# Polynomial-sketch attention and a cosine router: 36 blocks of tokens in place of 41, last parts of experts in shared blocks, and another order of the early work

## The chip, the cores and the metric

The kernel runs on one core of a Trainium2 chip. The core has a matrix engine (TensorE, PE in the profile), a vector engine (VectorE, DVE), a scalar engine (ScalarE, ACT), a general engine (GpSimd, POOL) and a queue engine for transfers (SyncE, SP). Matmuls read the on-chip memory SBUF and write the accumulation memory PSUM, in banks of 512 fp32 numbers per partition; every tile has up to 128 partitions. Measured is the time of one execution on the device in microseconds, lower is better. All data are fp32 unless a line says bf16.

## The reference

Two stages. The first is linear attention with a product sketch; its result is handed, token by token, to a router that sends each token to one of 8 experts, each a two-layer network.

```python
batch, n_heads, seq, head_dim = (4, 4, 1088, 32);  r = 8
def phi(x):                                   # 64 features of a row of 32
    a = einsum('rd,bhsd->bhsr', S1, x)
    b = einsum('rd,bhsd->bhsr', S2, x)
    return einsum('bhsi,bhsj->bhsij', a, b).reshape(..., r * r)
q_p, k_p = phi(q), phi(k)
kv  = einsum('bhsf,bhsd->bhfd', k_p, v)       # sum over all keys
z   = sum(k_p, axis=2)
x   = einsum('bhsf,bhfd->bhsd', q_p, kv) / (einsum('bhsf,bhf->bhs', q_p, z)[..., None] + 1e-6)
x   = x.transpose(0, 2, 1, 3).reshape(4352, 128)          # tokens

logits = normalized(x) @ normalized(expert_emb).T / tau   # 8 experts
expert_idx = argmax(logits, axis=1)
gate = softmax(logits)[expert_idx]
for e in range(8):                            # w1: 8 x 128 x 1024, w2: 8 x 1024 x 128
    out[mask_e] = gate * (relu(x[mask_e] @ w1[e]) @ w2[e])
```

How many tokens an expert gets is known only when the router has run.

## The kernel before

The two halves of the batch are m = 0 and m = 1. A half is cut into 17 tiles of 128 rows, in groups of 4, 4, 4 and 4 + 1. Everything is written as steps with a tick and a rank; the ticks are emitted in order, so every engine has a fixed order of work. In ticks 0 to 3 keys and queries of the first half are prepared, in 4 to 7 its results are formed beside the keys of the second half, and so on.

Loads, in the order of the transfer queue (k, q and v have different layouts: q is cut with its own stride):

```python
    for m in range(NM):
        k_sb[m] = rows_p.tile([P, H, 2, NK, D], F32, tag="rows", name=f"k{m}")
        q_sb[m] = rows_p.tile([P, H, NC, D], F32, tag="rows", name=f"q{m}")
        load_k(m, 0)
        if m == 0:
            load_q(0, 0, 8)
        load_v(m, 0)
        load_k(m, 1)
        if m == 0:
            nc.sync.dma_start(emb_sb[:], emb)
            nc.sync.dma_start(tau_sb[:], bass.AP(tensor=tau.tensor, offset=tau.offset, ap=[[0, E], [1, 1]]))
            load_q(0, 8, NC)
        load_v(m, 1)
        load_rest(m)
        load_q_rest(m)
    load_q(1, 0, NC)
```

w2 of an expert comes in pieces of 512 B (128 numbers):

```python
    def load_w2(e):
        nc.sync.dma_start(w2_sb[:, e], w2[e].rearrange("(f p) d -> p f d", p=P))
```

The sketch of a tile (two linear maps of each row) and the products. `u` chooses the half of the output partitions. Keys and queries of a tick share one PSUM bank, of which there is one:

```python
    def sketch(ps, t, n):

        for u in range(2):
            r = slice(u * HALF, (u + 1) * HALF)
            if n == 1:
                nc.tensor.matmul(ps[r, :H * 2 * R], t[:, r], Sblk.rearrange("p g r -> p (g r)"), start=True, stop=True)
            else:
                for h in range(H):
                    nc.tensor.matmul(ps[r].rearrange("p (g h r) -> p g h r", h=H, r=2 * R)[:, :, h],
                                     t[:, h * P + u * HALF:h * P + (u + 1) * HALF], Sblk, start=True, stop=True)
        return ps[:, :n * H * 2 * R].rearrange("p (g t r) -> p g t r", t=2, r=R)

    def second(ab, n, tag):
        b = tile_of(n, [P, n * H, R], tag)
        nc.scalar.copy(b, ab[:, :, 1])
        return b

    def features(ab, b, n, tag):
        t = tile_of(n, [P, n, H, R * R], tag)
        nc.vector.tensor_mul(t.rearrange("p j h (i k) -> p (j h) i k", i=R),
                             ab[:, :, 0].unsqueeze(3).broadcast_to([P, n * H, R, R]),
                             b.unsqueeze(2).broadcast_to([P, n * H, R, R]))
        return t

    def ab_bank(tick, n):

        if (tick, n) not in ab_ps:
            ab_ps[tick, n] = ps_small()[:, :2 * P] if n == 1 else ps_one("ab")
        return ab_ps[tick, n]
```

The sum over keys, and the query side: the products `qp` are turned (`tr_qp`) and, for the first half, kept turned in the place that w2 of experts 4 to 7 gets later (`held`):

```python
                    for p in range(2):
                        for u in range(2):
                            h = 2 * p + u
                            vo = v_rest[m][i][:, h] if rest else v_sb[m][:, h, c]
                            to_ones = (H - h) * D if rest else ((H - h) * 2 * NK - c) * D
                            nc.tensor.matmul(
                                acc[m][u * HALF:(u + 1) * HALF, i, p], s["kp"][:, c - c0, h],
                                bass.AP(tensor=vo.tensor, offset=vo.offset,
                                        ap=[list(vo.ap[0]), [to_ones, 2], [1, D]]),
                                start=p == 0 and c == 0, stop=rest, skip_group_check=True)
...
        def tr_qp():
            ps = ps_big() if n > 1 else ps_small().rearrange("p (b n) -> p b n", b=2)
            for j in range(n):
                for p in range(2):
                    nc.tensor.transpose(ps[:, p, j * P:(j + 1) * P],
                                        s["qp"][:, j, 2 * p:2 * p + 2].rearrange("p h f -> p (h f)"), ident)
            s["qpT"] = held[:, c0 // 4] if m == 0 and n > 1 else tile_of(n, [P, 2, w], "qpT")
            nc.scalar.copy(s["qpT"], ps[:, :, :w])

        def nd():
            ps = ps_big().rearrange("p b (u n) -> p (b u) n", u=2) if n > 1 else ps_small().unsqueeze(1)
            W = 2 * COLS
            for j in range(n):
                for i in range(2):
                    for p in range(2):
                        nc.tensor.matmul(
                            ps[i * HALF:(i + 1) * HALF, j, p * W:(p + 1) * W],
                            s["qpT"][:, p, j * P + i * HALF:j * P + (i + 1) * HALF],
                            kz[m][:, i, p].rearrange("p h d -> p (h d)"), start=True, stop=True)
            s["hs"] = ps[:, :n, :2 * W].rearrange("p n (h d) -> p n h d", h=H)
```

The router finds each token's expert and place, `mark` and `table` build the lists of tokens by block, and `write` stores the rows of x in device memory, in one buffer for the first half and one for all. Blocks of 128 tokens belong to one expert each. Every expert can leave one block partly filled, so their number is

```python
NBLK = (N + E * (P - 1)) // P                              # (4352 + 8*127)//128 = 41
EARLY = (NM * NC * P // 2 - E * (P - 1) + P - 1) // P      # 10, known from the first half alone
LATE = NBLK - EARLY                                        # 31
```

A block fetches its rows by an indirect gather, turns them, copies the weights of its expert (chosen by a register) to a fixed place, and runs two layers:

```python
    def turn(i):
        ps = ps_small()
        nc.tensor.transpose(ps[:, :P], xs[i][:, :DM], ident)
        xT[i] = work.tile([P, P], F32, tag="xTb", name="xTb")
        nc.vector.tensor_copy(xT[i], ps[:, :P])

    def weights(i):
        t, j = of(i)

        both = (mybir.EngineType.DVE, mybir.EngineType.Activation)
        e = nc.values_load(exp_i[t][0:1, j:j + 1], engines=both[:2 - t], min_val=0, max_val=E - 1,
                           skip_runtime_bounds_check_because="a count of experts, clamped to the last one")
        wb[i] = rows_p.tile([P, 2, F], F32, tag="rows", name="wb")
        nc.vector.tensor_copy(wb[i][:, 0], w1_sb[:, bass.ds(e, 1)].rearrange("p o f -> p (o f)"))
        w2 = w2_sb[:, bass.ds(e, 1)].rearrange("p o f d -> p (o f d)")
        if t == 0:
            nc.scalar.copy(wb[i][:, 1], w2)
        else:
            nc.vector.tensor_copy(wb[i][:, 1], w2)
...
    def up(i):
        ps = ps_big()
        hT[i] = work.tile([P, 2, 512], F32, tag="kp", name="hT")
        x, w = xT.pop(i), wb[i][:, 0]
        for u in range(2):
            for j in range(4):
                f = 4 * u + j
                nc.tensor.matmul(ps[:, u, j * P:(j + 1) * P], w[:, f * P:(f + 1) * P], x, start=True, stop=True)
        nc.scalar.activation(hT[i], ps, ACT.Relu)
...
    def down(i):
        ps = ps_one(("acc", "ab")[i % 2])[:, :DM]
        h, w = hT.pop(i).rearrange("p u n -> p (u n)"), wb.pop(i)[:, 1].rearrange("p (f d) -> p f d", d=DM)
        for f in range(NF):
            nc.tensor.matmul(ps, h[:, f * P:(f + 1) * P], w[:, f], start=f == 0, stop=f == NF - 1)
        y = work.tile([P, DM], F32, tag="y", bufs=3, name="y")
        nc.scalar.activation(y, ps, ACT.Copy, scale=gate.pop(i)[:, 0:1])
        xs.pop(i)
        t, j = of(i)
        nc.gpsimd.indirect_dma_start(
            out=out[:, :], out_offset=bass.IndirectOffsetOnAxis(ap=dst_i[t][:, j:j + 1], axis=0),
            in_=y[:], in_offset=None, bounds_check=N - 1, oob_is_err=False)
```

From tick 10 on, each tick has one block: up(i), then the tick's other work, then turn(i+1), share(i), down(i-1), weights(i+2). All 41 blocks run; a block without tokens writes nothing.

## Time and profile before

| | |
|---|---|
| time, median of 3 runs | 257.07 us (255.0 to 257.88) |
| span of the profiled execution | 253.9 us, 6275 instructions |
| mean granted TensorE clock | 0.954 of full |
| bytes moved | 24.30 MB in 22174 packets, 18629 of them under 2 KB |

The costliest groups of instructions, from the page (line, engine, operation, output <- inputs, count, busy us, mean ns of one, idle time before and its releaser):

```profile
L767 PE MATMUL ps_big<-xTb,wb 128*128 128x128 f32 x656 | 82.0, 279 | 3.1 <-DVE xTb L744 2.2
...
L782 PE MATMUL ps_acc<-wb,hT 128*128 128x128 f32 x336 | 41.0, 275 | 0.0
...
L753 DVE COPY wb<-w_sb 128x1024 f32 x41 | 28.6, 698 | 13.8 <-issue 12.8
...
L367 DVE TENSOR_TENSOR kp<-ps_ab,kb 128x1024 f32<-128x1024 f32 x8 | 9.7, 1211 | 15.0 <-ACT kb L362 9.8
```

An fp32 matmul of this kernel shows as two matmul instructions, so a layer of a block (8 matmuls) is 16 of them. Matmuls are pipelined: the mean duration (279 ns) is the way of one through the array, and the pace is read from the starts of successive ones. Of groups that are merged in the order of time, the duration runs from the first start to the last end. Idle time is put down to the event that came last.

### The profile page before, as it was taken

To read this page: it belongs to the slowest core of one execution; us is meant where nothing else is said; L and a number is where in the kernel's file an instruction comes from. 1 tells how busy PE (TensorE), PEld (TensorE's weight loads), DVE (VectorE), ACT (ScalarE), POOL (GpSimd) and SP (SyncE) were. 2 spreads that over 40 slices of the span, in tenths; PEclk is the share of its full clock that TensorE was granted. 3 is DMA by queue.
4 is the path that set the end of the run, shared out by engine and by line. 5 is a ranking of instruction groups with operands and counts; after the bars stand their busy time and mean duration, and the time that the engine had idled before them with its cause. 6 is when DMAs were issued, how large, how long until landed. Compare 5 with 4: busy or idle time off the path is not lost. (4 is left out here: it accounts for less than half of the span.)

```text
span 253.9 us, 6275 instructions
## 1 busy us (share of the span) xinstructions
PE 223.2 (88%) x2455; PEld 214.1 (84%) x2455; DVE 134.2 (53%) x399; ACT 118.1 (47%) x307; POOL 100.7 (40%) x115
## 2 busy tenths in 40 slices
PE   7679498986877989999999999999999999999930
PEld 6467397876766888999999999999999999999930
DVE  4285504899754788773454455455545544554300
ACT  2426225646552776656635444543444354345410
POOL 3001000312081335455654655565556556552330
PEclk9999869999795899999999999999999999999995
DMA  5969999939620021311111111101111111120000
GB/s 142 268 136 348 232 321 343 361 139 271 227 49 12 14 92 46 110 34 40 37 32 34 35 35 43 40 26 35 39 32 44 34 38 32 35 42 25 7 0 0
DMA packets 22174, 24.30 MB, mean 96 GB/s; under 512 B 5306, under 2 KB 18629, under 8 KB 22145
## 3 DMA queue, kind: packets, MB, share of 16 engines
q1 hardware_dynamic: 19520, 18.79, 25.2%
q0 software_dynamic: 2624, 5.11, 8.4%
q8 instruction: 19, 0.31, 0.5%
q14 instruction: 11, 0.08, 0.1%
HBM read 18.09 MB, written 6.26 MB: 96 GB/s over the span
## 5 line engine op out<-in xcount | busy, mean ns | idle before, releaser
L767 PE MATMUL ps_big<-xTb,wb 128*128 128x128 f32 x656 | 82.0, 279 | 3.1 <-DVE xTb L744 2.2
L767 PEld LDWEIGHTS ps_big<-xTb,wb 128*128 128x128 f32 x656 | 78.2, 195 | 3.7 <-DVE xTb L744 2.4
L787 POOL DMA_INDIRECT out_dram<-y,dst_i x41 | 46.6, 1137 | 59.3 <-ACT y L784 47.4
L768 ACT ACTIVATE hT<-ps_big 128x1024 f32<-128x1024 f32 x41 | 42.0, 1024 | 58.5 <-PE ps_big L767 45.3
L736 POOL DMA_INDIRECT xs<-rows,src_i x41 | 40.9, 998 | 21.7 <-DVE xg L500 9.8
L782 PE MATMUL ps_acc<-wb,hT 128*128 128x128 f32 x336 | 41.0, 275 | 0.0
L782 PEld LDWEIGHTS ps_acc<-wb,hT 128*128 128x128 f32 x336 | 39.2, 192 | 0.0
L782 PE MATMUL ps_ab<-wb,hT 128*128 128x128 f32 x320 | 39.0, 275 | 0.0
L782 PEld LDWEIGHTS ps_ab<-wb,hT 128*128 128x128 f32 x320 | 37.4, 192 | 0.0
L753 DVE COPY wb<-w_sb 128x1024 f32 x41 | 28.6, 698 | 13.8 <-issue 12.8
L512 POOL TENSOR_TENSOR xg<-ssq,half_c 128x4 f32<-128x4 f32 (+1 forms) x10 | 9.4, 942 | 46.9 <-ACT sq L510 42.1
L775 DVE TENSOR_SCALAR gate<-gate 128x1 f32<-128x1 f32 x41 | 6.2, 152 | 38.2 <-ACT hT L768 22.9
L758 DVE COPY wb<-w_sb 128x1024 f32 x31 | 21.3, 686 | 0.0
L744 DVE COPY xTb<-ps_t 128x128 f32<-128x128 f32 x41 | 11.9, 290 | 15.8 <-PE ps_t L742 12.7
L367 DVE TENSOR_TENSOR kp<-ps_ab,kb 128x1024 f32<-128x1024 f32 x8 | 9.7, 1211 | 15.0 <-ACT kb L362 9.8
L367 DVE TENSOR_TENSOR qp<-ps_ab,qb 128x1024 f32<-128x1024 f32 x8 | 9.8, 1220 | 9.3 <-ACT kb L362 5.0
L784 ACT ACTIVATE y<-ps_acc,gate 128x128 f32<-128x128 f32 x21 | 7.7, 368 | 12.4 <-PE ps_acc L782 11.9
L784 ACT ACTIVATE y<-ps_ab,gate 128x128 f32<-128x128 f32 x20 | 7.4, 368 | 11.3 <-PE ps_ab L782 10.3
L510 ACT ACTIVATE sq<-xg 128x128 f32<-128x128 f32 x34 | 10.5, 310 | 3.8 <-DVE xg L500 2.9
L742 PE MATMUL ps_t<-ident,xs 128*128 128x128 f32 x41 | 11.4, 278 | 1.0 <-ACT qT L342 0.8
L772 ACT ACTIVATE probs<-xs 128x8 f32<-128x8 f32 x41 | 11.9, 291 | 0.0
L756 ACT COPY wb<-w_sb 128x1024 f32 x10 | 10.4, 1047 | 1.8 <-DMA w_sb<-in_moe_w_dram 1.3
(178 smaller groups left out, 256.8 us busy)
## 6 DMA issues: line engine op xcount, KB each, us to landing
w_sb<-in_moe_w_dram SPq DMA_DIRECT2D x16, 512.0 KB, 8.4
k<-in_k_dram SPq DMA_DIRECT2D x4, 512.0 KB, 5.2
v<-in_v_dram SPq DMA_DIRECT2D x4, 512.0 KB, 7.0
rows<-xg SPq DMA_DIRECT2D x3, 616.5 KB, 3.9
rows<-xg SPq DMA_DIRECT2D x3, 548.0 KB, 2.8
q<-in_q_dram SPq DMA_DIRECT2D x2, 544.0 KB, 7.1
xs<-rows,src_i POOLq DMA_INDIRECT x41
out_dram<-y,dst_i POOLq DMA_INDIRECT x41
```

Of the source, the lines that this page charges most:

```text
L367: nc.vector.tensor_mul(t.rearrange("p j h (i k) -> p (j h) i k", i=R), ab[:, :, 0].unsqueeze(3).broadcast_to([P, n * H, R, R]), b.unsqueez ...
L736: nc.gpsimd.indirect_dma_start(out=xs[i][:], out_offset=None, in_=rows[t][:, :], in_offset=bass.IndirectOffsetOnAxis(ap=src_i[t][:, j:j + ...
L742: nc.tensor.transpose(ps[:, :P], xs[i][:, :DM], ident)
L744: nc.vector.tensor_copy(xT[i], ps[:, :P])
L753: nc.vector.tensor_copy(wb[i][:, 0], w1_sb[:, bass.ds(e, 1)].rearrange("p o f -> p (o f)"))
L758: nc.vector.tensor_copy(wb[i][:, 1], w2)
L767: nc.tensor.matmul(ps[:, u, j * P:(j + 1) * P], w[:, f * P:(f + 1) * P], x, start=True, stop=True)
L768: nc.scalar.activation(hT[i], ps, ACT.Relu)
L772: nc.scalar.activation(p, xs[i][:, DM:DM + E], ACT.Exp, scale=xs[i][:, ROW - 1:], accum_out=gate[i])
L782: nc.tensor.matmul(ps, h[:, f * P:(f + 1) * P], w[:, f], start=f == 0, stop=f == NF - 1)
L784: nc.scalar.activation(y, ps, ACT.Copy, scale=gate.pop(i)[:, 0:1])
L787: nc.gpsimd.indirect_dma_start(out=out[:, :], out_offset=bass.IndirectOffsetOnAxis(ap=dst_i[t][:, j:j + 1], axis=0), in_=y[:], in_offset=N ...
```

## The change

- **Fewer blocks.** Whole blocks of an expert as before; what is left of each expert is cut in halves of 64 tokens. A left-over of more than 64 fills a block of its own; the others share a block two by two: the first 64 rows belong to one expert, the last 64 to another. 38 blocks are provided; blocks 0 to 35 always run, the last two stand in a branch (`tc.If`) that is entered only if the count of blocks asks for it. With these inputs it is passed.
- **Shared blocks** (numbers 30 to 33) have two sets of weights. Their first layer has four matmuls of 64 columns out of 64 for one of 128 out of 128, on alternating halves of the output partitions, their second two of 64 output rows.
- **One layout for loads.** k, v and q have the same cut, k and q of the first half come first, in alternation. w2 comes with 8 rows per partition, in pieces of 4 KB; for that the first layer's weights are copied with a step of 8 numbers.
- **Queries held unturned.** The query products of the first half are kept as they are and turned in ticks 4 to 7, not in 0 to 3.
- **Halved sketches.** The loop over output halves is the inner one; sketches of keys and queries have banks of their own, two of each in the first ticks.
- **Own ticks.** Most steps of the second half get a tick and rank of their own, the first block's turn stands directly before its first layer, reciprocals of the router move to GpSimd, some copies to ScalarE, the tables of the second part are built over more ticks, and the rows go to one buffer.
- The scatters of results are declared independent of each other.

The core of the diff, with cuts marked by `...`:


```diff
-NBLK = (N + E * (P - 1)) // P
+
+NBLK = ((N + E * (HALF - 1)) // HALF + 1) // 2
+FULL = (N // HALF - E) // 2
...
+SHARED = E // 2
+PAIRS = FULL - EARLY
 AHEAD = 4
+USUAL = N // P + 2
+NO_KEY = 4096.0
...
+            for c in range(0, NK, NK // 2):
+                load(k_sb, k, 0, 0, c, c + NK // 2)
+                load(q_sb, q, 0, 0, c, c + NK // 2)
+            load(k_sb, k, 0, 1)
+            load(q_sb, q, 0, 1)
+            load(v_sb, v, 0, 0)
+            load(v_sb, v, 0, 1)
+            load_rest(0)
...
-        nc.sync.dma_start(w2_sb[:, e], w2[e].rearrange("(f p) d -> p f d", p=P))
+
+        nc.sync.dma_start(w2_sb[:, e], w2[e].rearrange("(p f) d -> p f d", p=P))
...
-        for u in range(2):
-            r = slice(u * HALF, (u + 1) * HALF)
-            if n == 1:
-                nc.tensor.matmul(ps[r, :H * 2 * R], t[:, r], Sblk.rearrange("p g r -> p (g r)"), start=True, stop=True)
-            else:
-                for h in range(H):
+
+        for h in range(H if n > 1 else 1):
+            for u in range(2):
+                r = slice(u * HALF, (u + 1) * HALF)
+                if n == 1:
...
+            if tick >= 2 * n_g and n == 1:
+                ps = ab_ps[tick, 4][:, 1:]
+            elif n == 1:
+                ps = ps_small()[:, :2 * n * HALF].rearrange("p (u n) -> p u n", u=2)
+            elif tick < n_g:
+                ps = ps_big()
+            else:
+
+                ps = ps_one("acc" if tick == 2 * n_g + 1 else "ab").rearrange("p (u n) -> p u n", u=2)
+            ab_ps[tick, n] = ps
+        return ab_ps[tick, n][:, u, :n * HALF]
...
+            t = held[:, c0 // 4].rearrange("p (j h f) -> p j h f", j=4, h=H) if m == 0 and n > 1 else None
+            s["qp"] = features(s["ab"], s["b"], n, "qp", t)
...
-            nc.vector.tensor_scalar_add(d, d, NORM_EPS)
-            nc.vector.reciprocal(d, d)
+            nc.gpsimd.tensor_scalar_add(d, d, NORM_EPS)
+            nc.gpsimd.tensor_tensor(out=d, in0=d, in1=minus[:, :n], op=ALU.pow)
...
+        (nc.scalar.copy if 4 <= i <= 8 else nc.vector.tensor_copy)(xT[i], ps[:, :P])
+
+    def first_layer(to, e):
+
+        nc.vector.tensor_copy(to.rearrange("p (f q) -> p f q", f=NF),
+                              w1_sb[:, bass.ds(e, 1)].rearrange("p o (q f) -> p (o f) q", f=NF))
...
+                if not two(i):
+                    nc.tensor.matmul(ps[:, u, j * P:(j + 1) * P], w[:, f * P:(f + 1) * P], x, start=True, stop=True)
+                    continue
+                for b, wh in enumerate((w, second_weights(i, 0))):
+                    for c in range(2):
+                        r = slice(c * HALF, (c + 1) * HALF)
+                        nc.tensor.matmul(ps[r, u, j * P + b * HALF:j * P + (b + 1) * HALF],
+                                         wh[:, f * P + c * HALF:f * P + (c + 1) * HALF], x[:, b * HALF:(b + 1) * HALF],
+                                         start=True, stop=True)
...
+            for b, wh in enumerate((w, second_weights(i, 1).rearrange("p (f d) -> p f d", d=DM))):
+                nc.tensor.matmul(ps[b * HALF:(b + 1) * HALF], h[:, f * P + b * HALF:f * P + (b + 1) * HALF], wh[:, f],
+                                 start=f == 0, stop=f == NF - 1, skip_group_check=True)
...
+        tc.declare_no_dep(d.ins, group="out", reason="no two blocks have a row in common")
+        tc.add_to_no_dep_group("out", d.ins)
...
+    put(1, 20.5, lambda: weights(0))
+    put(1, 30.5, lambda: turn(0))
...
+    n_late = nc.values_load(late["n"][:, :], min_val=0, max_val=LATE,
+                            skip_runtime_bounds_check_because="a count of blocks, of which there are no more")
+    with tc.If(n_late > USUAL - EARLY):
+        put = put_at(-1)
+        for i in range(USUAL, NBLK):
+            put(0, 0, lambda i=i: fetch(i))
+            if i < USUAL + 2:
+                put(0, 1, lambda i=i: weights(i))
+        put(0, 2, lambda: turn(USUAL))
+        in_ticks(USUAL, NBLK, 0)
+        emit()
```

## The prediction

> **What bounds the kernel now.** I read the busy shares and the slices of the span first, then windows of 10 us, then the order of time at four places.
>
> ```profile
> PE 223.2 (88%) x2455; PEld 214.1 (84%) x2455; DVE 134.2 (53%) x399; ACT 118.1 (47%) x307; POOL 100.7 (40%) x115
> ...
> PE   7679498986877989999999999999999999999930
> ...
> PEclk9999869999795899999999999999999999999995
> DMA  5969999939620021311111111101111111120000
> ```
>
> TensorE is the busiest engine, but unevenly. From slice 15 (95 us) to slice 37 it is full; before that it has holes, and its granted clock dips in three of them. The windows put numbers on both halves (columns: PE, PEld, DVE, ACT, POOL busy, granted clock, DMA share, GB/s):
>
> ```profile
> 20.00:30.00 10.00, 5.85 (x100) 5.01 (x97) 6.60 (x15) 3.78 (x13) 1.21 (x3) 0.97 1.07 297
> 30.00:40.00 10.00, 9.85 (x125) 8.70 (x125) 0.26 (x1) 3.92 (x9) 0.00 (x0) 0.69 1.10 313
> ...
> 70.00:80.00 10.00, 6.83 (x74) 5.75 (x73) 6.13 (x17) 4.44 (x13) 6.24 (x6) 0.84 0.16 39
> ...
> 160.00:170.00 10.00, 10.00 (x92) 10.00 (x91) 5.41 (x14) 4.07 (x12) 5.53 (x6) 1.00 0.14 37
> ```
>
> At 160 us TensorE is full at full clock, VectorE half full: only less TensorE work helps there. Summing PE over the first ten windows gives 79.8 of 100 us: 20 us idle. The clock below 1 in 30:40, 60:70, 70:80 and 80:90 (0.69, 0.84, 0.84, 0.80) is worth 8.3 us more, of which I count 7 as lost work.
>
> The steady block, in order of time (start, duration):
>
> ```profile
> 116.50 1.95 PE L767 MATMUL ps_big<-xTb,wb 128*128 128x128 f32 x16
> ...
> 118.29 0.27 PE L742 MATMUL ps_t<-ident,xs 128*128 128x128 f32 x1
> ...
> 118.39 1.95 PE L782 MATMUL ps_acc<-wb,hT 128*128 128x128 f32 x16
> ...
> 120.18 1.95 PE L767 MATMUL ps_big<-xTb,wb 128*128 128x128 f32 x16
> ```
>
> One block to the next is 120.18 - 116.50 = 3.68 us; sixteen matmul instructions start over 1.79 us, 112 ns each. Blocks 10 to 40 run at this pace: block 10 starts at 120.18 + 2 x 3.68 = 127.5 us (the blocks from 116.50 on are numbers 7, 8, 9), and TensorE ends at about 243.5.
>
> The way to the first block:
>
> ```profile
> 65.62 24.97 SPq L620 DMA_DIRECT2D rows<-xg  x3
> ...
> 70.03 1.18 POOL L736 DMA_INDIRECT xs<-rows,src_i  x1 [9.83 <-DVE xg L500]
> ...
> 74.56 0.33 PE L742 MATMUL ps_t<-ident,xs 128*128 128x128 f32 x1 [0.81 <-ACT qT L342]
> ...
> 77.63 0.28 DVE L744 COPY xTb<-ps_t 128x128 f32<-128x128 f32 x1
> ...
> 77.96 3.78 PE L767 MATMUL ps_big<-xTb,wb 128*128 128x128 f32 x16 [2.21 <-DVE xTb L744]
> ```
>
> The gather waits for the rows to be written (the releaser shown, VectorE, had long been done), its data are turned at 74.6, and then VectorE, busy with the next query tile, copies them 3 us later. TensorE sits idle and comes back at half clock: 3.78 instead of 1.95 us.
>
> [...]
>
> ```profile
> 7.47 0.97 PE L356 MATMUL ps_ab<-Sblk,kT 128*64 128x64 f32 x16 [0.67 <-ACT kT L342]
> ...
> 43.76 1.15 PE L406 MATMUL ps_acc<-v,kp 128*64 128x64 f32 x32
> ```
>
> Both have 64 columns out of 64 moving ones. The sum over keys alternates its output half with every matmul: (1.15 - 0.22)/31 = 30 ns each. The sketch keeps one half for eight instructions: (0.97 - 0.22)/15 = 50 ns. (2) [...]The hole of 3.5 us before the transposes of k at 30.0 us is followed by doubled durations[...]; the one before 78 us is shorter, 2.2 us, and has the same effect. (3) [...]The contiguous weight copy takes 694 ns against 1211 for a two-source product of the same 1024 elements; no run yet shows a strided one.[...]
>
> **The change part by part.**
>
> 1. Blocks 41 to 36. The count is (4352 + 8 x 127)/128 = 41 before; now 38 are provided, 36 run and two lie in a branch that is passed. In the steady stretch: -5 x 3.68 = -18.4 us.
>
> 2. Four shared blocks. Up is 8 x 2 x 2 matmuls, two instructions each: 64 at 30 ns, since the output half alternates = 1.92 us instead of 1.79. Down is 32 instructions of 128 columns, 112 ns in pairs on two halves = 1.79. With the changes between whole and halved array I put +0.35 us each: +1.4 us. Their extra copies (0.69 on VectorE, 1.05 on ScalarE) fit under 3.68 us: VectorE has 0.69 x 2 + 0.29 + 0.31 = 2.0 us a block, 2.7 with them.
>
> 3. First layer in another order: w1 read with a step of 8. By (3) it stays at 0.7 us. If it falls to 1211 ns, VectorE has 2.5 us a block and 3.7 in a shared one: still no bound in the steady part. The second layer's packets grow from 512 B to 4 KB; in the slices where DMA is full that helps, but the tiles it delays aren't the releasers of TensorE.
>
> 4. Sketches with alternating halves: 256 instructions x (50 - 30) = -5 us of TensorE, all before 90 us. On the path only partly; counted inside 5.
>
> 5. Early ticks. Before, one sketch bank serves k and q, so a tick is sketches (1.9), copies (0.5), two products (2.4): the products of ticks 0 to 3 start at 11.1, 15.8, 20.9, 26.7, a pitch of 5. Now two double banks serve them, the transposes of the query products are put off to ticks 4 to 7, and k and q lead in the DMA queue. Then VectorE's 2.4 us bounds a tick, TensorE needs 0.9 + 1.0 + 1.0 = 2.9; I take 3.3. VectorE's constants (2.3 us) now go ahead of the first product. Ticks 0 to 3 end near 22 instead of 30 us, and the first query matmul of the first half, at 41.2 before, follows the key sums by about 5 us: near 27 to 30. Ticks 4 to 7 took 17 us from there (41.2 to 58.3) and gain a transpose and a copy of 1 us each, which the gap-filled engines can hold: first half finished at 46 to 49 instead of 58.3.
>
> 6. From there to the first block: 78.0 - 58.3 = 19.7 us before. The row write leaves ahead of the marks, reciprocals move to GpSimd, the first turn stands directly before the first block, so the 3.1 us between turn and copy go, and about 2 us of the write's start. I take 15: first block at 61 to 64, choosing 66 for slips (loads landing late, half clock).
>
> 7. Ten early blocks cost 36.8 us; the rest of the second half's queries took 127.5 - 78.0 - 36.8 = 12.7 us before. With less half clock, fewer sketches and some of it done ahead I put 10. Block 10 starts at 66 + 36.8 + 10 = 113 instead of 127.5: -14.5 us.
>
> 8. The end. TensorE ends at 243.5, the span at 253.9:
>
> ```profile
> 241.59 1.95 PE L782 MATMUL ps_acc<-wb,hT 128*128 128x128 f32 x16
> ...
> 243.58 0.37 ACT L784 ACTIVATE y<-ps_acc,gate 128x128 f32<-128x128 f32 x1 [1.42 <-PE ps_acc L782]
> 245.32 0.98 POOL L787 DMA_INDIRECT out_dram<-y,dst_i  x1 [1.90 <-issue]
> ```
>
> The last scatter starts 1.4 us after its data (243.95): it waits for the scatter before it. Declared independent: -1.4. The count of blocks must be loaded into every engine and a branch taken: I guess +2.5, partly under the scatter's landing. Net +1.
>
> Sum: -18.4 + 1.4 - 14.5 + 1 = -30.5 us. From 257.1 to 226.6, say 227.
>
> **Rivals.** (a) Only the blocks count: the early stage is held by the loads (DMA share 1.07 and 1.10 from 20 to 40 us) or by VectorE, which is busy 8 of 10 us at 90:110. Then -18.4 + 1.4 + 1 = -16: 241 us. For it: the tables of the second part get some twenty small VectorE instructions more, and the copies of the strided layer may take 1.2 us. Against it: TensorE's waits before 60 us are for ScalarE and VectorE, not for DMA (the longest DMA wait is 0.75 us), and sum to 20 us. (b) The branch is dear[...]. Then +5 on my sum: 232. (c) The new ticks work as meant: first block at 61, no half clock, 8 us of queries beside the early blocks. Then 220. (d) Late table ready too late: its fetches come only two ticks (7 us) ahead of block 10, against five before. A gather took 70.03 to 74.56, so one fits, but a stall with a half-clock restart would cost 3 to 5 us: 231.
>
> **Range and chances.** The floor is the work: 223.2 - 7 - 5 - 18.4 + 1.4 = 194 us of TensorE, plus 10.4 + 1 of tail, plus 2.5 of a run's time over the span, is 208; with 10 to 30 us of idle and half clock, 218 to 238. I take 217 to 240, the upper end being rival (a). For the time to stay within 2% (over 252) the early stage would have to lose 11 us beside the blocks' gain. Faster 0.94, same 0.03, slower 0.03.
>
> **What would show it.** Right: 32 x 16 = 512 matmul instructions for the ordinary first layers and 4 x 64 = 256 for the shared ones; 3.68 us per ordinary block and about 4 per shared; sketches of 16 in about 0.7 us; the first block's matmuls at 61 to 66 us at full clock; product pitch of 3.3 us in ticks 0 to 3. Wrong: shared blocks at 5 us or more (halves not concurrent), holes in TensorE at the first blocks or at block 10, VectorE full between 60 and 115 us, a weight copy of 1.2 us with TensorE waiting for it, more than 14 us between TensorE's end and the span's.

## The result, and the profile after

| | before | changed kernel |
|---|---|---|
| time, median (range, runs) | 256.03 us (253.83 to 257.88, 4) | 228.18 us (226.21 to 230.79, 4) |
| ratio, 95% interval | | 0.887 [0.878, 0.896] |
| the same pair on another chip | 255.39 us (7 runs) | 224.94 us (223.46 to 225.61, 4), 0.883 [0.874, 0.892] |

Two of the four executions of the changed kernel, the profiled one (span 229.0 us, the first profile) among them, fell in a slower state, which the ratio leaves out, so the stages are read in the profile of the repeat (span 222.9 us), called the second profile. Its page, busy times and slices:

```profile
PE 200.5 (90%) x2554; PEld 190.4 (85%) x2554; DVE 143.2 (64%) x392; ACT 113.9 (51%) x296; POOL 112.2 (50%) x116
...
PE   8989969988679999989999999999999999999920
...
PEclk9999997999999999999999999999999999999995
DMA  5969899983010311400011111111111111100000
```

TensorE lost 22.7 us of busy time. Two of its three clock dips are gone. Counted from 0, slice 8 (to 50 us) is the last that is full of transfers; before, slices 9 and 10 (57 to 70 us) were busy once more. The windows, with the columns of those of before (PE, PEld, DVE, ACT, POOL busy, granted clock, DMA share, GB/s):

```profile
20.00:30.00 10.00, 9.58 (x186) 8.46 (x183) 6.35 (x13) 5.61 (x17) 0.00 (x0) 1.00 0.96 306
30.00:40.00 10.00, 7.78 (x122) 6.85 (x122) 4.55 (x13) 5.00 (x18) 1.77 (x2) 0.83 1.02 407
...
60.00:70.00 10.00, 6.99 (x75) 6.10 (x76) 8.78 (x20) 7.03 (x21) 6.79 (x7) 1.00 0.13 33
70.00:80.00 10.00, 9.65 (x120) 9.25 (x119) 6.52 (x23) 7.79 (x26) 7.67 (x7) 1.00 0.20 72
...
160.00:170.00 10.00, 10.00 (x92) 10.00 (x91) 5.88 (x14) 4.69 (x12) 6.48 (x6) 1.00 0.15 42
```

20 to 30 us, where TensorE was busy 5.85 us, is now nearly full; 30 to 40 us, where the loads now run at 407 instead of 313 GB/s, has a hole of its own. The steady stretch is as before. The way to the first block (order of time: start, duration, idle before):

```profile
52.84 1.94 SPq L655 DMA_DIRECT2D rows<-xg  x2
...
57.93 1.23 POOL L846 DMA_INDIRECT xs<-rows,src_i  x1 [5.50 <-DVE rc L527]
...
60.78 0.33 PE L852 MATMUL ps_t<-ident,xs 128*128 128x128 f32 x1 [1.15 <-DMA xs<-rows,src_i]
61.15 0.29 DVE L855 COPY xTb<-ps_t 128x128 f32<-128x128 f32 x1 [0.34 <-PE ps_t L852]
```

The copy now follows the turn by 0.37 us, where it stood 3 us behind it, and the first block's matmuls begin at 61.49 us and take 2.05 us, full clock. In the first profile the same place reads:

```profile
64.02 0.48 PE L852 MATMUL ps_t<-ident,xs 128*128 128x128 f32 x1 [1.85 <-DMA xs<-rows,src_i]
64.88 3.78 PE L902 MATMUL ps_big<-xTb,wb 128*128 128x128 f32 x16 [0.38 <-DVE xTb L855]
```

3.4 us later and at half clock (3.78 instead of 2.05 us): this is most of the 6.1 us between the two spans. An ordinary block and the shared ones in the chain of waits of the second profile (start, duration):

```profile
183.56 1.79 PE ps_big L902 x16
...
187.25 2.02 PE ps_big L907 x64
...
189.52 1.79 PE ps_ab L925 x16
191.31 2.02 PE ps_big L907 x64
```

Sixty-four small matmul instructions take 2.02 us, about 30 ns each, where the sketch of the kernel before, on one half for eight instructions, took 50. In the second layer of a shared block the matmuls of the two halves start in pairs, 0.01 us apart (193.51 and 193.52, 193.67 and 193.68 us): the halves do run side by side. Block to block it is 187.25 - 183.56 = 3.69 for an ordinary one and 191.31 - 187.25 = 4.06 for a shared one.

| place in the span, us | before | predicted | second profile |
|---|---|---|---|
| key products of ticks 0 to 3 start | 11.1, 15.8, 20.9, 26.7 | pitch 3.3 | 8.7, 11.1, 14.2, 19.3 |
| first query matmuls of the first half | 41.2 | 27 to 30 | 26.0 |
| first block's first layer | 78.0 | 61 to 64, counted as 66 | 61.5 |
| block 10 | 127.5 | 113 | 113.0 |
| last result leaves ScalarE | 243.95 | | 213.5 |
| end of span | 253.9 | | 222.9 |

### The profile page after: what moved, and what is told of

It reads as the page before. It is cut to its first block, busy times and chain, and to the rows that moved or that the text cites. A ratio compares the mean times of both kernels' runs of the same rounds, so it can differ in the third digit from the quotient of the medians.

```text
span 229.0 us, 6455 instructions
## 1 busy us (share of the span) xinstructions
PE 205.7 (90%) x2554; PEld 195.2 (85%) x2554; DVE 143.1 (63%) x392; ACT 114.0 (50%) x296; POOL 113.7 (50%) x116
## 4 chain that ended last, share of the span: by engine, by line
PE 59%; DVE 15%; issue 9%; POOL 4%; SPq 4%; DMA 4%; ACT 1%; DVEq 0%; POOLq 0%; ACTq 0%
PE ps_big L902 21%; PE ps_ab L925 11%; PE ps_acc L925 10%; POOL out_dram L934 3%; PE ps_big L516 3%; PE ps_big L502 3%; SPq L122 2%; DMA k_rest<-in_k_dram 2%; PE ps_t L713 2%; DVE wb L859 2%; PE ps_acc L426 2%; PE ps_t L852 2%; PE ps_big L907 2%; DVE xg L528 1%; DMA xs<-rows,src_i 1%
## 5 line engine op out<-in xcount | busy, mean ns | idle before, releaser
L902 PE MATMUL ps_big<-xTb,wb 128*128 128x128 f32 x512 | 65.0, 281 | 2.2 <-DVE wb L859 0.9
L902 PEld LDWEIGHTS ps_big<-xTb,wb 128*128 128x128 f32 x512 | 61.3, 196 | 3.8 <-ACT y L931 1.0
L846 POOL DMA_INDIRECT xs<-rows,src_i x36 | 41.2, 1145 | 21.8 <-issue 15.1
L859 DVE COPY wb<-w_sb 128x1024 f32 x36 | 39.7, 1104 | 12.5 <-issue 11.8
L925 PE MATMUL ps_ab<-wb,hT 128*128 128x128 f32 x256 | 32.5, 282 | 0.0
L925 PEld LDWEIGHTS ps_ab<-wb,hT 128*128 128x128 f32 x256 | 31.3, 200 | 0.0
L925 PE MATMUL ps_acc<-wb,hT 128*128 128x128 f32 x256 | 31.3, 275 | 0.0
L925 PEld LDWEIGHTS ps_acc<-wb,hT 128*128 128x128 f32 x256 | 29.8, 192 | 0.0
L874 DVE COPY wb<-w_sb 128x1024 f32 x26 | 17.9, 687 | 0.0
L516 PEld LDWEIGHTS ps_big<-kz,qpT 128*64 128x64 f32 x256 | 10.6, 147 | 5.9 <-issue 4.1
L516 PE MATMUL ps_big<-kz,qpT 128*64 128x82 f32 x256 | 11.9, 250 | 1.4 <-ACT qpT L508 1.3
L508 ACT COPY qpT<-ps_big 128x1024 f32<-128x1024 f32 x8 | 8.1, 1013 | 6.1 <-PE ps_big L502 5.9
```

The lines of the kernel that those rows point to most:

```text
L516: nc.tensor.matmul(ps[i * HALF:(i + 1) * HALF, j, p * W:(p + 1) * W], s["qpT"][:, p, j * P + i * HALF:j * P + (i + 1) * HALF], kz[m][:, i ...
L846: nc.gpsimd.indirect_dma_start(out=xs[i][:], out_offset=None, in_=rows[:2 * S if t == 0 else N], in_offset=bass.IndirectOffsetOnAxis(ap=sr ...
L859: nc.vector.tensor_copy(to.rearrange("p (f q) -> p f q", f=NF), w1_sb[:, bass.ds(e, 1)].rearrange("p o (q f) -> p (o f) q", f=NF))
```

## The experiments

Twelve kernels. Unless said otherwise an edit is made in the changed kernel, and "the changed kernel" is its repeat, 224.94 us. The runs are spread over four chips, on which the kernel before takes 252.7 to 255.4 us (medians). Each ratio is to the kernel before on the same chip; between chips, a difference of 1 or 2 us in the times alone shows little. e1 to e4 ran on one chip, e5 to e8 on a second, e9 to e11 on a third, e12 on a fourth.

**The changed kernel again** (e1_control), no edit.

> The changed kernel once more. In its first profile TensorE waited from 31.3 to 34.0 us for nothing that the profile names, and then ran at half clock until 40. Theory A (the wait is an instruction fetch that stands behind the weight loads, so its length depends on luck): executions without it are 3 to 5 us shorter, a span near 224 to 225, and a profile of one shows no wait of over 1 us near the 961st TensorE instruction. Theory B (the wait belongs to the program): it is in every profile with the same length. Ratio to the kernel before 0.88 to 0.895.

224.94 us. TensorE's hole at 30 us is there again, after the same instruction, 2.2 us long instead of 2.8. It is no accident of one execution, but its length changes.

**Only fewer blocks** (e2_before_36). The kernel before, with its first 36 blocks alone; the tokens of the last five blocks are left out.

```diff
+    RUN = 36
-    for i in range(NBLK + 1):
+    for i in range(RUN + 1):
...
-        if i < NBLK:
+        if i < RUN:
             put(0, 30, lambda i=i: up(i))
...
```

> The kernel before, with only the first 36 of its 41 blocks run (the rows of the last five are left out of the output). If the blocks are worth what the prediction gave them, 5 x 3.68 = 18.4 us: 256 - 18.4 = 237.6, ratio 0.928, and TensorE's end moves from 243.5 to 225. Then the new ticks bring the remaining 10 us or so of the measured 29. Rival: the early stage gains the larger part, and 36 blocks alone give less than 15 us (ratio above 0.942).

236.62 us (234.73 to 238.17) against 255.39; ratio 0.927 [0.918, 0.936]. That is 18.8 us for five blocks, and the price of a block in the steady stretch (5 x 3.68 = 18.4) was the right one. The other 11.7 us, down to 224.94, belong to the rest of the change.

**No branch** (e3_no_branch). The count's load and the two blocks in the branch, which these inputs do not need, are left out.

```diff
-    n_late = nc.values_load(late["n"][:, :], min_val=0, max_val=LATE, ...)
-    with tc.If(n_late > USUAL - EARLY):
-        ...
```

> The changed kernel without the branch and the load of the count of blocks into the engines (blocks 36 and 37 are left out; they are passed with these inputs). If the passed branch costs what the prediction put there, 2.5 us partly under the last scatter's landing: 1 to 2.5 us less, ratio to the changed kernel 0.989 to 0.996. Rival[...]: 4 us or more. Other rival (all of it lies under the last scatter's landing): no difference, within 0.5 us.

224.44 us (223.38 to 225.09), 0.880 [0.872, 0.888]: by the time alone no difference. The end of the trace shows one. The second profile (span 222.9), then the one without a branch (span 223.2), in order of time:

```profile
213.10 0.37 ACT L931 ACTIVATE y<-ps_ab,gate 128x128 f32<-128x128 f32 x1 [1.42 <-PE ps_ab L925]
213.75 0.98 POOL L934 DMA_INDIRECT out_dram<-y,dst_i  x1 [0.80 <-ACTq L1038]
```

```profile
214.81 0.37 ACT L931 ACTIVATE y<-ps_ab,gate 128x128 f32<-128x128 f32 x1 [1.42 <-PE ps_ab L925]
215.45 0.98 POOL L934 DMA_INDIRECT out_dram<-y,dst_i  x1 [0.80 <-ACT y L931]
```

From the end of the last result to the end of the span it is 222.9 - 213.47 = 9.4 us with the branch (9.4 to 9.5 in the seven other profiles that have it and write rows as the change does) and 223.2 - 215.18 = 8.0 without, in one profile. By that reading the branch and the load of its count cost 1.4 us. This profile's first block came 1.7 us late (63.16 us), which hides it; over four runs the medians differ by 0.5 us only, less than their ranges.

**One bank for the early sketches** (e6_one_bank).

```diff
-            elif tick < n_g:
-                ps = ps_big()
```

> Changed kernel with the key and query sketches of the first four ticks in one bank of PSUM as before. Theory A (the second bank is what lets the products of the early ticks follow each other): products come 4.5 to 5 us apart again, the first query matmul at 31 to 34 us instead of 26.9, the first block 3 to 6 us later, 3 to 5 us slower (about 228). Theory B (the spacing is set by the loads of k and by VectorE, the bank adds nothing): first query matmul within 1 us of 26.9, time within 1 us.

227.75 us (227.20 to 228.99), 0.897 [0.890, 0.905], 2.8 us slower. Its key products in order of time:

```profile
8.95 1.22 DVE L377 TENSOR_TENSOR kp<-ps_ab,kb 128x1024 f32<-128x1024 f32 x1
13.11 1.22 DVE L377 TENSOR_TENSOR kp<-ps_ab,kb 128x1024 f32<-128x1024 f32 x1 [1.80 <-ACT qb L371]
19.40 1.23 DVE L377 TENSOR_TENSOR kp<-ps_ab,kb 128x1024 f32<-128x1024 f32 x1 [3.93 <-PE ps_acc L424]
24.81 1.22 DVE L377 TENSOR_TENSOR kp<-ps_ab,kb 128x1024 f32<-128x1024 f32 x1 [0.16 <-issue]
```

The mean pitch is 5.3 us again, and the first query matmuls come at 31.35 instead of 26.00. Part of this is the clock: it is at half from 12.9 to 19.8 us in this profile (mean granted clock 0.967, in the second profile 0.979). It was full there in the kernel before, whose pitch was 5.2. Of the 5.4 us, 2.0 are left at the first block (63.51) and 3.1 at block 10 (116.13). The hole of 2.2 us at 30 us and the clock dip behind it are not there in this profile; that they give back the rest fits the sum and was not tried alone.

**Sketches in the old order** (e7_sketch_order).

```diff
-        for h in range(H if n > 1 else 1):
-            for u in range(2):
+        for u in range(2):
+            for h in range(H if n > 1 else 1):
```

> Changed kernel with the loops over halves and heads in the sketches in the old order[...]. Each group of 16 takes 0.97 us again instead of 0.66 to 0.69. Theory A (TensorE's time up to the first block is on the path): 16 groups x 0.3 = 4.8 us more of TensorE, 3 to 5 us slower. Theory B (the sketches lie beside VectorE and loads in the ticks): 0 to 1.5 us slower.

226.43 us (224.61 to 227.99), 0.893 [0.886, 0.901]. Most groups take 0.91 to 0.97 us again, yet the first block starts at 61.71 and block 10 at 113.36 (61.49 and 113.00 with the halved sketches). This profile is of the shortest of the four runs; without the longest the median is 226.2 us, 1.3 us over the changed kernel on another chip, with ranges that overlap. Where the 5 us of TensorE went in this profile is seen at the hole. The second profile:

```profile
29.42 0.98 PE L502 MATMUL ps_big<-ident,w_sb 128*128 128x128 f32 x7
32.62 0.37 PE L502 MATMUL ps_big<-ident,w_sb 128*128 128x128 f32 x1 [2.22 <-issue]
32.93 2.46 PE L516 MATMUL ps_big<-kz,qpT 128*64 128x82 f32 x32
```

With sketches in the old order:

```profile
33.49 0.27 PE L502 MATMUL ps_big<-ident,w_sb 128*128 128x128 f32 x1 [1.42 <-issue]
33.69 1.36 PE L516 MATMUL ps_big<-kz,qpT 128*64 128x82 f32 x32
```

TensorE comes later to the same place, waits 1.42 instead of 2.22 us, and goes on at full clock (1.36 instead of 2.46 us for the query matmuls). Between these two profiles, what the faster sketches gain is spent in a longer wait and a clock dip. But the dip is not tied to the faster sketches, nor to the longer wait: e8, which has the faster sketches, waits longer still and goes on at full clock. Its chain of waits:

```profile
32.15 2.49 issue
34.64 0.27 PE ps_big L502
34.91 1.29 PE ps_big L516 x32
```

What the traces show of the dip is in the last section.

**Marks of the late table side by side** (e4_late_table). TensorE adds up the token lists of the second part from marks of 32 lists by 36 tiles. The change, in a detail that its list above leaves out, stores them list by list, so that the matmul of one tile reads every 36th number; here they lie tile by tile, as before.

```diff
-                s["hit"] = work.tile([P, n, w], BF16, ...)
-                s["col"] = work.tile([P, 2, n, w], BF16, ...)
+                s["hit"] = work.tile([P, w, n], BF16, ...)
+                s["col"] = work.tile([P, w, 2, n], BF16, ...)
...
-                nc.tensor.matmul(s["ps"], row[:, :, t], s["col"].rearrange("p d n w -> p (d n) w")[:, :, t], ...)
+                col = (s["col"].rearrange("p d n w -> p (d n) w")[:, :, t] if which == 0
+                       else s["col"][:, t].rearrange("p d n -> p (d n)"))
+                nc.tensor.matmul(s["ps"], row[:, :, t], col, ...)
```

> The changed kernel with the late table stored tile by tile again, so that the 34 matmuls that sum it read their moving rows without a step. In the changed kernel they take 4.3 us (step of 36 numbers, 72 bytes), before 2.2, and the clock falls to half behind them for 3.4 us. Theory A (the step halves the pace of the moving rows, and the slow stream also lets the clock fall): sums in 2.2 us, full clock behind them, 3 to 4 us less, ratio to the changed kernel about 0.985; VectorE's two products become 1.26 instead of 0.76 us. Theory B (VectorE bounds this stretch, its 1 us more shows up): sums faster, but no more than 1 us less in all.

223.40 us (222.63 to 224.29), 0.878 [0.870, 0.886], 1.5 us under the changed kernel on the same chip, though the intervals overlap. The group of the sums, in the second profile and here:

```profile
L713 PE MATMUL ps_t<-col,row 128*128 128x64 bf16 x34 | 4.3, 303 | 0.0
```

```profile
L721 PE MATMUL ps_t<-col,row 128*128 128x64 bf16 x34 | 2.2, 223 | 0.0
```

With the step of 72 B in the moving operand the sums take twice as long here. Block 10 in the second profile and here:

```profile
113.00 1.95 PE L902 MATMUL ps_big<-xTb,wb 128*128 128x128 f32 x16
```

```profile
111.66 1.95 PE L910 MATMUL ps_big<-xTb,wb 128*128 128x128 f32 x16
```

From the first block to block 10 it is 111.66 - 61.74 = 49.9 instead of 51.5 us; of the 2.1 us saved, 0.6 go to a wait before block 8 (0.90 instead of 0.31), since VectorE's products in this order take 1.36 us each instead of 0.76 and its weight copy stands behind them. The half clock of 3.4 us that followed the sums in the first profile is in neither of these two.

**Plain order of the weights** (e8_plain_w1). Copy in its own order, w2 in pieces of 512 B as before.

```diff
-        nc.sync.dma_start(w2_sb[:, e], w2[e].rearrange("(p f) d -> p f d", p=P))
+        nc.sync.dma_start(w2_sb[:, e], w2[e].rearrange("(f p) d -> p f d", p=P))
...
-        nc.vector.tensor_copy(to.rearrange("p (f q) -> p f q", f=NF),
-                              w1_sb[:, bass.ds(e, 1)].rearrange("p o (q f) -> p (o f) q", f=NF))
+        nc.vector.tensor_copy(to, w1_sb[:, bass.ds(e, 1)].rearrange("p o f -> p (o f)"))
```

> Changed kernel with the first layer's weights copied in their own order (one run of columns) and the second layer's rows loaded in the old pieces of 512 B. The copy falls from 1.1 to 0.69 us. Theory A (the copy lies beside TensorE's 3.68 us a block): within 0.5 us. Theory B (VectorE is near full where late experts' routing and blocks overlap): 1 to 2 us faster. Theory C (the larger pieces of the second layer's load were worth something): second-layer loads take longer, 1 to 3 us slower.

229.60 us (228.14 to 230.55), 0.902 [0.894, 0.910]: 4.7 us slower, although the copy falls from 1111 to 702 ns and VectorE's busy time from 143.2 to 127.8 us. In its chain of waits:

```profile
52.98 7.25 DMA rows<-xg
60.23 0.70 DVE wb L859
...
61.53 2.83 DMA xs<-rows,src_i
...
65.27 3.78 PE ps_big L901 x16
```

The token rows take 7.25 us to land, in the second profile 2.8 to 4.2. The transfers are still full (1.01, 349 GB/s) between 53 and 56 us, where they are not in the second profile; the windows, second profile first, columns as above:

```profile
53.00:56.00 3.00, 2.83 (x51) 2.43 (x47) 2.92 (x7) 1.00 (x3) 0.00 (x0) 1.00 0.60 214
```

```profile
53.00:56.00 3.00, 2.83 (x58) 2.43 (x54) 2.86 (x10) 1.30 (x4) 0.00 (x0) 1.00 1.01 349
```

Then the first block starts late and at half clock.

**Rows from another queue** (e10_rows_gpsimd), and **plain weights with rows from another queue** (e11_plain_rows). Both have this edit, the second on top of the last experiment:

```diff
-            nc.sync.dma_start(rows[at:at + SK].rearrange(...), xg[g][:, :NK])
+            nc.gpsimd.dma_start(rows[at:at + SK].rearrange(...), xg[g][:, :NK])
...
-                    nc.sync.dma_start(rows[at:at + HALF], ...)
+                    nc.gpsimd.dma_start(rows[at:at + HALF], ...)
```

> Changed kernel with the token rows written to memory from GpSimd's queue instead of SyncE's, where they are issued behind the loads of the second layer's weights. Theory A (the weight loads on SyncE's queue hold the rows, and the rows the first block): first block's matmuls at 60 to 62 us in every profile at full clock, 0 to 3 us faster than the changed kernel (222 to 225). Theory B (VectorE's routing chain sets the first block, the rows are there in time): within 0.7 us. Theory C: [...]1 to 3 us slower.

> The kernel with contiguous first-layer copy and second-layer pieces of 512 B (4.5 us slower than the changed one) with the rows written from GpSimd's queue. Theory A (its loss is the rows waiting behind more and smaller weight packets on SyncE's queue): 2.5 to 4.5 us of it come back (224 to 226.5), first block at 60 to 63 us. Theory B (its loss is the loads as such, all later, or lies in the blocks): 229 to 230, first block still at 65.

Rows from another queue: 225.25 us (224.44 to 226.60), 0.897 [0.887, 0.907]: no gain over the changed kernel. First block at 61.87. In the changed kernel the rows were in time and VectorE's routing sets the first block; and 0.8 us are lost at the end, where it is 10.2 us from the last result to the end instead of 9.4, in all three kernels with this edit.

Plain weights with it: 226.18 us (225.27 to 227.06), 0.900 [0.891, 0.910]. The first block:

```profile
62.69 2.05 PE L901 MATMUL ps_big<-xTb,wb 128*128 128x128 f32 x16 [0.38 <-DVE xTb L855]
```

It stands at 62.69 us and full clock, where e8 had 65.27 and half clock, and block 10 at 113.18 instead of 117.13. By the times 3.4 of the 4.7 us come back; but the two ran on different chips, and their ratios, 0.902 and 0.900, do not show it. What carries the reading is the two traces and the pair on one chip: with the rows on their own queue, plain weights cost 0.9 us (226.18 against 225.25), with ranges that overlap. So the larger pieces of w2 gain through the rows that queue behind them, and little in themselves.

**Weights read with a step by TensorE** (e9_step_weights). Copy in its own order, large pieces; the weight load takes every eighth column.

```diff
...
-                    nc.tensor.matmul(ps[...], w[:, f * P:(f + 1) * P], x, ...)
+                    nc.tensor.matmul(ps[...], w.rearrange("p (q f) -> p f q", f=NF)[:, f], x, ...)
...
```

> Changed kernel, but the first layer's weights are copied in their own order (VectorE, one run of columns) and TensorE loads every eighth column of the copy as its stationary matrix; the second layer's large pieces stay. Theory A (the weight load takes a step of 32 B at the same pace, 192 ns, and the slow copy costs TensorE no more than the one wait of 0.9 us): copy 0.69 us, block 3.68 us, time 0 to 1.5 us under the changed kernel (223 to 225). Theory B (a step costs TensorE as it does in the late table's sums): blocks of 4.5 us or more, 15 us or more slower.

296.98 us (295.42 to 298.54), 1.180 [1.167, 1.194]. Order of time:

```profile
173.40 4.00 PE L901 MATMUL ps_big<-xTb,wb 128*128 128x128 f32 x16
...
177.34 1.95 PE L924 MATMUL ps_acc<-wb,hT 128*128 128x128 f32 x16
179.13 3.98 PE L901 MATMUL ps_big<-xTb,wb 128*128 128x128 f32 x16
```

The layer that loads with a step of 32 B takes 4.00 us, the other 1.95; a block is 179.13 - 173.40 = 5.73 us. The step is far cheaper in VectorE's copy (1111 instead of 698 ns), which lies beside the matmuls.

**Weight loads spread out** (e5_paced). Each expert's weights wait for a small write of VectorE, one expert a tick.

```diff
+    def load_weights(e):
+        nc.vector.memset(w1_sb[0:1, e, 0:1], 0.0)
         nc.sync.dma_start(w1_sb[:, e], w1[e])
...
+        load_w2(e)
...
+    for e in range(1, E):
+        put_at(ND_AT[0][0] + e)(0, 54.5, lambda e=e: load_weights(e))
```

> Weight loads issued one expert at a time, each behind a one-element VectorE write at the tick that needs the DMA no longer, instead of all at once. Theory A (TensorE's gap of 1.9 to 3.0 us at 30 to 34 us is the fetch of the next 16 KB of instructions, standing behind the weight loads): the gap falls to 1 us or less, TensorE's clock stays full up to the first block, 2 to 4 us faster than the changed kernel (about 221). Theory B (the gap is a wait of TensorE for data that has nothing to do with the loads): gap unchanged, time within 1 us. Theory C: the last weights now come too late for the first blocks: the first block's matmuls wait for w2_sb or w1_sb and the time grows by 1 to 4 us.

231.69 us (231.23 to 234.09), 0.915 [0.906, 0.924], 6.8 us slower. The hole is there, 2.2 us. The windows explain why this says nothing about theory A (29 to 32 us, columns as above), and the chain of waits shows theory C:

```profile
29.00:32.00 3.00, 2.03 (x40) 1.83 (x40) 1.93 (x5) 2.09 (x9) 0.61 (x1) 1.00 1.02 410
```

```profile
54.91 5.03 DMA rows<-xg
...
65.16 3.78 PE ps_big L905 x16
...
72.67 3.73 DMA w_sb<-in_moe_w_dram
```

At the hole the transfers are as full as before, now with the loads of k, q and v. And weights that come late meet the rows on their way, delay the first block, and then hold up the weight copy on ScalarE, which stands idle for 2.2 of the 3.73 us.

**Together** (e12_best). The table of e4, the rows of e10, and one step of the table behind the weight copy:

```diff
-    put(3, 76, high)
+    put(3, 79.5, high)
```

> Changed kernel with the late table's marks side by side for TensorE (sums 2.2 instead of 4.3 us), the token rows written from GpSimd's queue, and the first product of the late table behind the weight copy in VectorE's order, so that block 8 no longer waits 0.9 us for its weights. Theory A (the gains lie in different stages and add): 222 to 223.5, that is 1.5 to 3 us under the changed kernel; block 10's matmuls at 110 to 111.5 us instead of 113.0. Theory B (what the sums save, VectorE's longer products take back): 224 to 225, block 10 at 112.5 or later.

224.85 us (224.31 to 226.73, 6 runs), 0.893 [0.886, 0.900]. By the time this is theory B. Block 10 starts at 112.15, between the two theories and no better than with the table alone (111.66): the wait before block 8 is gone, but block 7 waits 1.18 us instead of 0.87, and the end is 0.8 us longer. The fastest kernel measured stays the table alone (ratio 0.878).

## Why the prediction came out right

Predicted were 227 us and a sum of -30.5 us. The spans of before and of the second profile differ by -31.0: -14.5 up to block 10, -15.9 from there to the last result, -0.5 at the end. The blocks and their price were right, and so was the way in which the early stage gains; that the sum came so near is also luck, since errors of 4.5 and 4.7 us cancel (6 and 7).

1. *Five blocks, -18.4.* Right, shown alone by e2 (-18.8).
2. *Shared blocks, +0.35 each.* Right: 4.06 - 3.69 = 0.37. The share in it of changes between whole and halved array was the author's estimate; in the second profile a layer of whole matmuls ahead of halved ones holds TensorE for 1.88 us (189.36 to 191.24) instead of 1.79. From block 10 to the last result that gives -18.4 + 1.5 = -16.9; the other 1.0 us are small waits, the largest seen 0.3 us before block 11.
3. *First layer's copy stays at 0.7 us, and larger packets delay no releaser of TensorE.* Wrong in both. The group in the second profile:

```profile
L859 DVE COPY wb<-w_sb 128x1024 f32 x36 | 40.0, 1111 | 12.3 <-issue 11.3
```

1111 ns, against 698 before, near the 1211 that the prediction named as the other case. That it stays at 0.7 us was the author's estimate; the trace of before shows the contiguous copy alone. TensorE waited for such a copy once, 0.87 us (0.54 at the same block in e11, whose copy is short, for ScalarE). The other half of the step looked at the wrong releaser: whatever w2's tiles release, the rows queue behind them, and the traces of e8 and e11 put the first block at 65.27 and 62.69 us. In the total the error did no harm: the larger packets helped the rows, and step 6 had counted a later first block than the one that came.
4. *Sketches, -5 us of TensorE.* Size right (0.97 to 0.66 us a group); on the path it is worth 0.4 us at block 10 in the profile of e7, and 1.3 us by its time, which its range does not set apart from nothing.
5. *Early ticks.* The pitch is 2.4, 3.0 and 5.2 us where 3.3 was said; ahead of the last, VectorE waits 1.33 us for the norms of the router's expert vectors, a chain that goes back to the small rest of k (5.3 us of transfer):

```profile
17.84 0.14 DVE L310 TENSOR_SCALAR emb_ss<-emb_ss 8x1 f32<-8x1 f32 x1 [1.33 <-POOL emb_ss L305]
```

First query matmuls at 26.0 (27 to 30); the first half ends at 49.4 (46 to 49), by the VectorE sum that ended at 58.3 before. The banks carry the pitch: without them it is 5.3 (e6, in part at half clock). The hole at 30 us was not foreseen.
6. *First block at 61 to 64, counted as 66.* 61.5 us in the second profile, 64.9 and at half clock in the first. From the end of the first half it took 12.1 us, not 15; the slip that was counted for came in some executions only.
7. *Other work between first block and block 10, 10 us.* The term that was mis-sized: 113.0 - 61.5 - 36.8 = 14.7, more than the 12.7 of before. Steps 6 and 7 err by -4.5 and +4.7, so block 10 stands where it was said by luck. 1.6 of the 4.7 are the late table's sums, shown by e4: their marks were laid out anew, so that VectorE's products are short and TensorE reads with a step, 4.3 instead of 2.2 us. The prediction counted the table's instructions on VectorE and overlooked its layout. Two more terms stand in the traces. Two groups of query products are turned behind the first block (16 matmul instructions, 2.2 us), where before it was one (8, 1.1 us). And from the first block to block 10 TensorE is idle for 51.51 - 47.85 = 3.66 us, before for 49.59 - 47.44 = 2.15: the 0.87 for the copy is in it, and three waits between the first and the second block (0.46, 0.99 and 0.39 us), the longest for the copy of the turned queries.
8. *End: -1.4 + 2.5.* Sizes off, sum near: the last scatter starts 0.3 instead of 1.4 us after its data (-1.1), the branch costs 1.4 (e3), and the span's end after the last result moved from 9.95 to 9.43 us. In e2, which ends as the kernel before does, it is 9.2 us, so single profiles of that end differ by as much as this.

Of the rivals, (a) falls with block 10 at 113 us, (b) with the branch at 1.4 us, (d) with the order of time: TensorE goes into block 10 without a wait. (c), 220 us, had the right first block and too little work behind it. Against (a) the prediction named 20 us of TensorE's waits before 60 us, the longest DMA wait among them 0.75; in the trace these waits sum to 12.8 us before 60 us (20 before 100), and the longest for DMA is 0.64. The argument stands with the smaller numbers.

Not tried alone, and so not shown, are the shares of the loads' order, the queries held unturned, the first turn's place and the reciprocals on GpSimd in the 11.7 us that the blocks leave, and the gain of 1.1 us from the independent scatters, which is read from the trace.

## What to carry to other kernels

A faster stage pays only up to the next wait: of 5 us of TensorE, 0.4 were left at block 10 where two traces could be compared, since the rest ended in a hole and a clock dip. When a transfer's pieces or order are changed, look not only at who reads its data but at what queues behind it. And when a table or weight changes its layout, ask for every engine that reads it what the step costs: here it doubled the time of matmuls (4.3 instead of 2.2 us for the table's sums) and slowed a copy (1111 instead of 698 ns).

## What the runs showed of the hardware that was not expected

- **Steps cost TensorE twofold, on both operands tried.** A bf16 moving operand with a step of 72 B: 4.3 instead of 2.2 us for 34 matmuls (second profile and e4). An fp32 stationary operand with a step of 32 B: 4.00 instead of 1.95 us for 16 matmul instructions (e9).
- **The strided fp32 copy was slower on VectorE.** 1111 ns with a source step of 8 numbers (second profile) against 702 without (e8), for 1024 numbers per partition.
- **The clock changed on a grid of 3.413 us, and the length of a pause alone did not decide about it.** In the traces of before and of the first profile every stretch between two changes of the granted clock is a whole multiple of 3.413 us (before: 23.89, 6.83, 30.72, 3.41, 6.83, 6.83 and 163.84 us, that is 7, 2, 9, 1, 2, 2 and 48; first profile: 27.31, 6.83, 23.89, 6.83, 40.96, 3.41 and 109.23 us, that is 8, 2, 7, 2, 12, 1 and 32). Cut into windows along these multiples, the two traces have, up to the end of the matmuls, four windows at full clock in which TensorE stood idle for 1.98 to 2.88 us, and the window after each is at half clock; of eight with 1.08 to 1.41 us idle, one is followed by half clock. At the hole a pause of 2.22 us was followed by half clock (second profile) and one of 2.49 us was not (e8). Before the first block 1.74 us gave half clock in part of its first layer (e6, 3.25 us) and 1.81 us did not (e4, 2.05 us). One stretch at half clock, at 111.76 us of the first profile, follows a window without a pause; that window holds 28 of the 34 stepped sums of the late table.
- **A hole beside a fetch of instructions.** In five traces TensorE stops after the same instruction, for 1.42 to 2.77 us (first and second profile, e5, e7, e8). In the first profile 471 matmul instructions lie ahead of that place; a packet of 16,384 bytes of instructions starts on its way at 31.60 us, 0.33 us after the stop, and TensorE goes on at 34.04 us, while the data transfers are full (1.03, 414 GB/s from 31 to 34 us). In e6 TensorE goes through the same place without a pause (eight transposes from 34.77 us on, in 1.09 us). That the full transfers delay the packet is an argument and not shown: e5 was to show it and did not empty them in time.
- **Rows written from GpSimd's queue lengthen the end by 0.8 us** in all three kernels that do it; why was not tried.
